# Reading the moving columns of three matrix products from the last to the first

## The chip, the cores and the metric

The kernel runs on one core of one Trainium2 chip. The metric is the device time of one execution in microseconds (us), as the median of several runs; lower is better. Besides these runs there is one execution taken by the hardware profiler, and all rows shown here come from that one.

## The reference

Windowed attention with a distance bias feeds a channel mix (a feed-forward block with token shift). Cut to what matters:

```python
B, H, S, D = 4, 8, 768, 64            # attention; x has 512 features
x = attention(q, k, v)                # -> (B, S, 512)
x_prev = shift x by one token
xk = mu_k * x + (1 - mu_k) * x_prev
xr = mu_r * x + (1 - mu_r) * x_prev
k = maximum(xk @ w_k, 0)              # w_k: 512 x 1024
v = (k * k) @ w_v                     # w_v: 1024 x 512
r = sigmoid(xr @ w_r)                 # w_r: 512 x 512
return r * v
```

The channel mix runs over 4 x 768 = 3072 tokens.

## The kernel before

The tokens are cut into 24 tiles of 128; two tiles form a chunk of 256, and the channel mix runs once for each of the 12 chunks. A main loop goes over the tiles: it loads q, k and v, forms scores (L421 to L425), takes the exponential (L431), transposes it (L461), multiplies it by v (L486), and a few steps later puts the chunk's channel mix in small pieces (a Python generator, `run_ffn`) between the pieces of the attention of later tiles. The final order of the instructions on each engine is set when the program is built, by a planner that lays the work out along a timeline of its own estimates.

All products of the channel mix are in split form: each operand is a high part and a low part in the 4-byte type fp32r, and `three` (L527 to L530) adds three matmuls into one sum in PSUM: high x high, high x low, low x high. So each line, L528, L529 and L530, holds a third of the matmuls. There are three products:

- **kp** (L546 to L554): weights of w_k are held in the array, the tokens of `xk` move past it, 256 columns each time. One PSUM tile takes two such sums (2 x 256). Four tiles for a chunk.
- **z** (L532 to L538): 128 tokens of `xr` are held, the 512 columns of w_r move. Two tiles for a chunk.
- **vps** (L573 to L579): 128 tokens of `kkh`/`kkl` (the square of the rectified kp, high and low) are held, the 512 columns of w_v move. Two tiles for a chunk; in the last chunk the second tile is done in two halves of 256 columns.

The sums of all three share the pool `ps_f`, three PSUM tiles that are handed out in turn. They are read by these four instructions: ScalarE takes the rectified kp (L555), VectorE multiplies it by kp (L556), ScalarE takes the sigmoid of z (L568), VectorE multiplies vps by it (L580). L557 and L558 then split the square into the high and low part that vps needs; these read SBUF only. The results go out by DMA (L581).

Two lines outside the channel mix serve as yardsticks later: L230, which in the first 35 us multiplies an identity by 512 columns of plain fp32, and L262/L264, which test the weights' raw 8-byte words late in the kernel and read every second 4-byte word.

Of the kernel before, what the change touches and what calls it, by code (L numbers as in the profile page):

```python
# [14 lines left out]
AF = mybir.ActivationFunctionType  # L15
# [47 lines left out]
def tile_biased_attention_channel_mix(ctx: ExitStack, tc: tile.TileContext, qT, kT, v, n_sizes, mu_kr, w_k, w_v, w_r, q_rows, k_rows, v_rows, slopes, out):  # L63
    nc = tc.nc
    vec, act, pool, pe = nc.vector, nc.scalar, nc.gpsimd, nc.tensor
# [27 lines left out]
    wts = {}  # L93
# [56 lines left out]
    for h in range(H):  # L150
        c = -8.0 * 2.0 ** -(h + 1)
# [15 lines left out]
    for h in range(H):  # L167
        c = -8.0 * 2.0 ** -(h + 1)
# [72 lines left out]
    def range_load():  # L241
        n = len(words_again)
        if n == 20:
            return
        name, src, j = w_steps[n // 2]
        if n % 2:
            raw = p4k.tile([128, 512, 2], I32, tag="t4k", name=f"again_{n}")
        else:
            raw = q_pool.tile([128, 512, 2], I32, tag=("qh", "ql")[n // 2 % 2], name=f"again_{n}")
        at, o = divmod((j * 2 + n % 2) * 512 // 512 * 1024 + n % 1 * 1024, 2048 if name == "k" else 1024)  # L250
        nc.sync.dma_start(raw.rearrange("p n w -> p (n w)"), src[at * 128 : (at + 1) * 128, o : o + 1024])
        words_again.append(raw)

    def range_test(behind_vec, behind_act):
        n = tested[0]
        if n == len(words_again):
            return
        tested[0] += 1
        raw = words_again[n]
        low, top = raw[:, :, 0], raw[:, :, 1]  # L260
        with tc.issue_after(behind_vec.ins):
            vec.tensor_scalar(low, top, 27, 15, op0=ALU.logical_shift_right, op1=ALU.bitwise_and)  # L262
        with tc.issue_after(behind_act.ins):
            act.activation(top.bitcast(F32), low, AF.Abs, bias=middle, accum_out=odd[:, n : n + 1])  # L264

    def range_worst():
        vec.reduce_max(worst[:, 0:1], odd, axis=AX.X)
        row = ps_f.tile([128, 512], F32, name="row", tag="f")
        pe.matmul(row[0:1, 0:128], worst[:, 0:1], ident, start=True, stop=True)
        vec.reduce_max(worst[0:1, 1:2], row[0:1, 0:128], axis=AX.X)  # L270
# [22 lines left out]
    def weights_need(n):  # L293
        weights_go(n, n)
# [211 lines left out]
    def part(pool, tag, n):  # L506
        t = pool.tile([128, n * 256 + GAP.get(tag, 0)], F32R, name=tag, tag=tag)
        return t[:, 0 : n * 256].rearrange("p (a q) -> p a q", a=n)
# [15 lines left out]
    def channel_mix(xk, xr, out_rows, f_pool, f2_pool, ps_f, more=False, final=False):  # L524
        kkh, kkl = (part(f_pool, f"kk_{p}", 8) for p in ("hi", "lo"))

        def three(o, sh, sl, mh, ml, first, last):  # L527
            pe.matmul(o, sh, mh, start=first, stop=False)  # L528
            pe.matmul(o, sh, ml, start=False, stop=False)  # L529
            pe.matmul(o, sl, mh, start=False, stop=last)  # L530

        def z_of(i):  # L532
            z = ps_f.tile([128, 512], F32, name="z", tag="f")
            c = slice(i * 128, (i + 1) * 128)
            for k in range(4):
                three(z, xr[0][:, k, c], xr[1][:, k, c], *wts["r", k], k == 0, k == 3)
                yield
            sig = f2_pool.tile([128, 512], F32, name="sig", tag="f2")  # L538
            sigs.append((z, sig))

        sigs = []
        for fp in range(4):
            weights_need(4)
            ps = ps_f.tile([128, 512], F32, name="kp", tag="f")
            for u in range(2):
                f = slice((2 * fp + u) * 128, (2 * fp + u + 1) * 128)  # L546
                o = ps[:, u * 256 : (u + 1) * 256]
                for k in range(4):
                    hi, lo = wts["k", k]
                    three(o, hi[:, f], lo[:, f], xk[0][:, k, :], xk[1][:, k, :], k == 0, k == 3)  # L550
                    if k % 2:
                        yield
            kk = f2_pool.tile([128, 2, 256], F32, name="kk", tag="f2")
            pv = ps.rearrange("p (a q) -> p a q", a=2)  # L554
            act.activation(kk, pv, AF.Relu)  # L555
            vec.tensor_mul(kk, pv, kk)  # L556
            high = act.copy(kkh[:, 2 * fp : 2 * fp + 2, :], kk)  # L557
            rest = vec.tensor_sub(kkl[:, 2 * fp : 2 * fp + 2, :], kk, kkh[:, 2 * fp : 2 * fp + 2, :])  # L558
            if more:
                for i in range(3):  # L560
                    range_load()
                for i in range(3):
                    range_test(rest, high)
        weights_need(6)
        for i in range(2):
            yield from z_of(i)
        for z, sig in sigs:
            act.activation(sig, z, AF.Sigmoid)  # L568
        for i in range(2):
            c = slice(i * 128, (i + 1) * 128)  # L570
            sig = sigs[i][1]
            ends = (0, 256, 512) if final and i else (0, 512)
            for a, b in zip(ends, ends[1:]):  # L573
                vp = ps_f.tile([128, 512], F32, name="vps", tag="f")
                for f in range(8):
                    weights_need(7 + f // 2)
                    hi, lo = wts["v", f]
                    three(vp[:, a:b], kkh[:, f, c], kkl[:, f, c], hi[:, a:b], lo[:, a:b], f == 0, f == 7)
                    yield  # L579
                vec.tensor_mul(sig[:, a:b], vp[:, a:b], sig[:, a:b])  # L580
                nc.sync.dma_start(out_rows(i)[:, a:b] if final and i else out_rows(i), sig[:, a:b])  # L581
            if more and i == 0 and tested[0] == 20:
                range_worst()

    def ffn(c):
        xt = state["x", c]
        xk = mix(xt[:, :, 1:257], xt[:, :, 0:256], "k", p4k, f_pool, c < PLAN.get("MA", 1))
        xr = mix(xt[:, :, 1:257], xt[:, :, 0:256], "r", p4k, f_pool, c < PLAN.get("MA", 1))
        return channel_mix(xk, xr, lambda i: out[(2 * c + i) * 128 : (2 * c + i + 1) * 128, :], f_pool, f2_pool, ps_f, c >= 10, c == NCHUNK - 1)
# [84 lines left out]
    def wide():  # L674
        weights_any()
        with ExitStack() as g:
# [85 lines left out]
            with tc.For_i(0, B, 1) as b:  # L762
                for c in range(3):
                    xt = work.tile([128, 4, 257], F32, name="g_x", tag="g_x")
                    src = rows[ds(b, 1)].rearrange("b p a s -> p (b a) s")
                    if c:
                        nc.sync.dma_start(xt, src[:, :, 256 * c - 1 : 256 * c + 256])
                    else:
                        pool.memset(xt[:, :, 0:1], 0.0)
                        nc.sync.dma_start(xt[:, :, 1:257], src[:, :, 0:256])  # L770
                    xk = mix(xt[:, :, 1:257], xt[:, :, 0:256], "k", work, work)
                    xr = mix(xt[:, :, 1:257], xt[:, :, 0:256], "r", work, work)

                    def out_rows(i):
                        return rows_out[ds(b, 1), (2 * c + i) * 128 : (2 * c + i + 1) * 128, :].rearrange("b s d -> (b s) d")

                    for _ in channel_mix(xk, xr, out_rows, work, work4, ps_f):
                        pass
# [63 lines left out]
```

## Time and profile before

| | us |
|---|---|
| median of 3 runs | 501.81 |
| the three runs | 504.63, 501.81, 500.86 |
| the profiled execution | 499.25 |
| its span, first to last instruction | 497.5 |
| TensorE busy (matmuls) in the span | 485.3 |
| VectorE busy | 350.4 |
| ScalarE busy | 329.2 |
| GpSimd busy | 205.9 |

The span is what the trace shows in rows; the profiled execution's own time is 1.75 us longer and lies 0.5% below the median of the runs. Engines work side by side, so the busy times don't add up to the span. A matmul's row lasts longer than the distance to the next matmul's start, since they are pipelined: what a matmul costs TensorE is the distance from one start to the next.

### The profile page before, as it was taken

How to read it: one execution, taken by the hardware profiler on the slowest of the kernel's cores; microseconds unless marked ns; L12 is line 12 of the kernel's file. 1: busy time of each engine (PE TensorE's matmuls, PEld its weight loads, DVE VectorE, ACT ScalarE, POOL GpSimd, SP SyncE). 2: the span in 40 equal slices, each digit the busy share in tenths (PEclk: the TensorE clock that was granted, in tenths of full speed). 3: DMA queues.
4: the chain of work that ended last, by engine and by line, in shares of the span. 5: the costliest groups of instructions: out<-in, count | busy, mean ns of one | idle time of the engine just before them, and what ended most of it. 6: DMA issues, size and time to landing. Idle time of an engine off the chain costs nothing.

```text
span 497.5 us, 10274 instructions
## 1 busy us (share of the span) xinstructions
PE 485.3 (98%) x3614; PEld 431.7 (87%) x3614; DVE 350.4 (70%) x839; ACT 329.2 (66%) x842; POOL 205.9 (41%) x339
## 2 busy tenths in 40 slices
PE   7999999899999999999999999999999999999995
PEld 5687997698988998998998998998998998988984
DVE  7999996677677677677687676677678665456431
ACT  8899866346287578567478477577587587595450
POOL 4211047337355544554655645644655634203000
PEclk9999999999999999999999999999999999999999
DMA  7997331650615306405405405405505125674301
GB/s 253 366 313 306 80 83 40 155 138 5 167 31 148 94 17 166 108 1 164 124 6 149 119 1 159 133 2 141 148 2 131 56 52 172 195 254 169 135 35 51
DMA packets 22587, 60.59 MB, mean 122 GB/s; under 512 B 3296, under 2 KB 4576, under 8 KB 22016
## 3 DMA queue, kind: packets, MB, share of 16 engines
q1 hardware_dynamic: 22384, 59.85, 40.2%
q8 instruction: 31, 0.51, 0.4%
q14 instruction: 28, 0.23, 0.2%
q10 hardware_dynamic: 144, 0.00, 0.0%
HBM read 53.55 MB, written 6.29 MB: 120 GB/s over the span
## 4 chain that ended last, share of the span: by engine, by line
PE 88%; DVE 6%; ACT 2%; DMA 1%; issue 1%; POOL 0%; SPq 0%; DVEq 0%; POOLq 0%; ACTq 0%
PE kp L528 9%; PE kp L529 9%; PE kp L530 9%; PE vps L528 8%; PE vps L530 8%; PE vps L529 8%; PE av L486 7%; PE t L461 7%; PE z L528 4%; PE z L529 4%; PE z L530 4%; PE s L425 3%; PE s L424 3%; PE s L422 2%; PE s L421 2%; PE rest L230 1%
## 5 line engine op out<-in xcount | busy, mean ns | idle before, releaser
L449 POOL TENSOR_SCALAR e<-e,r 128x232 f32<-128x232 f32 (+1 forms) x144 | 68.6, 495 | 129.3 <-DVE r L443 91.9
L431 ACT ACTIVATE e<-e,nmax 128x232 f32<-128x232 f32 (+1 forms) x192 | 89.6, 469 | 34.2 <-DVE nmax L430 33.6
L528 PE MATMUL kp<-xk_hi,wk 128*128 128x256 f32 x384 | 108.0, 282 | 1.8 <-DVE sig L580 1.8
L529 PE MATMUL kp<-xk_lo,wk 128*128 128x256 f32 x384 | 107.3, 280 | 0.1
L530 PE MATMUL kp<-xk_hi,wk 128*128 128x256 f32 x384 | 107.2, 279 | 0.0
L430 DVE CUSTOM_DVE_ANT_0 e<-s,pat 128x232 f32<-128x232 f32 (+1 forms) x192 | 64.2, 373 | 28.0 <-PE s L425 25.9
L528 PE MATMUL vps<-wv,kk_hi 128*128 128x512 f32 (+1 forms) x200 | 76.8, 385 | 0.2 <-ACT wv L216 0.2
L530 PE MATMUL vps<-wv,kk_lo 128*128 128x512 f32 (+1 forms) x200 | 76.6, 383 | 0.0
L529 PE MATMUL vps<-wv,kk_hi 128*128 128x512 f32 (+1 forms) x200 | 76.4, 382 | 0.0
L528 PEld LDWEIGHTS kp<-xk_hi,wk 128*128 128x128 f32 x384 | 72.0, 188 | 3.0 <-DVE sig L580 2.1
L529 PEld LDWEIGHTS kp<-xk_lo,wk 128*128 128x128 f32 x384 | 72.1, 188 | 1.2 <-DVE xk_lo L521 0.8
L530 PEld LDWEIGHTS kp<-xk_hi,wk 128*128 128x128 f32 x384 | 72.1, 188 | 0.0
L465 ACT COPY et<-t 128x256 f32<-128x256 f32 (+1 forms) x176 | 53.3, 355 | 25.1 <-PE t L461 24.9
L461 PE MATMUL t<-ident,e 128*128 128x128 f32 x352 | 54.4, 275 | 0.4 <-ACT et L465 0.3
L556 DVE TENSOR_TENSOR kk<-kp,kk 128x512 f32<-128x512 f32 x48 | 32.9, 688 | 30.8 <-ACT kk L555 30.4
L558 DVE TENSOR_TENSOR kk_lo<-kk,kk_hi 128x512 fp32r<-128x512 f32 x48 | 36.5, 764 | 22.8 <-ACT kk_hi L557 22.0
L461 PEld LDWEIGHTS t<-ident,e 128*128 128x128 f32 x352 | 40.3, 136 | 6.1 <-ACT et L465 0.6
L557 ACT CAST kk_hi<-kk 128x512 fp32r<-128x512 f32 x48 | 29.7, 622 | 22.4 <-DVE kk L556 22.4
L530 PEld LDWEIGHTS vps<-wv,kk_lo 128*128 128x128 f32 x200 | 37.6, 188 | 7.5
L528 PEld LDWEIGHTS vps<-wv,kk_hi 128*128 128x128 f32 x200 | 37.6, 189 | 7.0 <-ACT wv L216 0.4
L529 PEld LDWEIGHTS vps<-wv,kk_hi 128*128 128x128 f32 x200 | 37.7, 189 | 6.5
L400 DVE TENSOR_TENSOR ql<-qraw,qh 128x1024 fp32r<-128x1024 f32 x18 | 32.8, 1825 | 14.5 <-POOL qh L297 14.5
(119 smaller groups left out, 1075.1 us busy)
## 6 DMA issues: line engine op xcount, KB each, us to landing
qraw<-in_qT_dram SPq DMA_DIRECT2D x36, 256.0 KB
kraw<-in_kT_dram SPq DMA_DIRECT2D x36, 256.0 KB
out_dram<-sig SPq DMA_DIRECT2D x23, 256.0 KB
va<-in_v_dram SPq DMA_DIRECT2D x20, 240.0 KB
vb<-in_v_dram SPq DMA_DIRECT2D x20, 208.0 KB
w<-in_w_k_dram SPq DMA_DIRECT2D x4, 1024.0 KB
w<-in_w_v_dram SPq DMA_DIRECT2D x4, 1024.0 KB
again<-in_w_k_dram SPq DMA_DIRECT2D x8, 512.0 KB
```

The source lines that it names most:

```text
L400: vec.tensor_sub(ql, s["qr"], qh)
L430: biased[n, hp] = vec.tensor_tensor_reduce(out=e[:, :w], in0=o, in1=p[:, h, :], op0=ALU.add, op1=ALU.min, scale=-0.125, scalar=3.0e38, acc ...
L431: act.activation(e[:, :w], e[:, :w], AF.Exp, bias=s["nmax"][:, h : h + 1], scale=-1.0, accum_out=s["sum"][:, h : h + 1])
L449: pool.tensor_scalar(e[:, :w], e[:, :w], r[:, u : u + 1], 1.0, op0=ALU.mult, op1=ALU.mult)
L461: s["turned"] = pe.transpose(pt[0:p, c : c + 128], e[:, k * 128 : k * 128 + p], ident)
L465: act.copy(dst, pt[0:p, k * 256 : k * 256 + 256].rearrange("p (u q) -> p u q", u=2)[:, :, q:128])
L486: pe.matmul(o, vt[:, h * 64 : (h + 1) * 64], et[0:p, c : c + 128 - q], start=k == 0, stop=k == nb - 1)
L528: pe.matmul(o, sh, mh, start=first, stop=False)
L529: pe.matmul(o, sh, ml, start=False, stop=False)
L530: pe.matmul(o, sl, mh, start=False, stop=last)
L556: vec.tensor_mul(kk, pv, kk)
L558: rest = vec.tensor_sub(kkl[:, 2 * fp : 2 * fp + 2, :], kk, kkh[:, 2 * fp : 2 * fp + 2, :])
```

## The change

The moving operand of every matmul of the channel mix is read from its last column to its first (`[:, ::-1]`, a step of -1 element). The sums therefore stand in PSUM in reverse order of columns, and the four instructions that read these sums read them backwards too, so that everything that is written to SBUF has the order it had. Number and sizes of instructions, the operands held in the array, the buffers and the DMAs are as before.

```diff
@@ z_of
-                three(z, xr[0][:, k, c], xr[1][:, k, c], *wts["r", k], k == 0, k == 3)
+                three(z, xr[0][:, k, c], xr[1][:, k, c], wts["r", k][0][:, ::-1], wts["r", k][1][:, ::-1], k == 0, k == 3)
@@ kp
-                    three(o, hi[:, f], lo[:, f], xk[0][:, k, :], xk[1][:, k, :], k == 0, k == 3)
+                    three(o, hi[:, f], lo[:, f], xk[0][:, k, ::-1], xk[1][:, k, ::-1], k == 0, k == 3)
@@
-            pv = ps.rearrange("p (a q) -> p a q", a=2)
+            pv = ps.rearrange("p (a q) -> p a q", a=2)[:, :, ::-1]
             act.activation(kk, pv, AF.Relu)
             vec.tensor_mul(kk, pv, kk)
@@
-            act.activation(sig, z, AF.Sigmoid)
+            act.activation(sig, z[:, ::-1], AF.Sigmoid)
@@ vps
-                    three(vp[:, a:b], kkh[:, f, c], kkl[:, f, c], hi[:, a:b], lo[:, a:b], f == 0, f == 7)
+                    three(vp[:, a:b], kkh[:, f, c], kkl[:, f, c], hi[:, a:b][:, ::-1], lo[:, a:b][:, ::-1], f == 0, f == 7)
                     yield
-                vec.tensor_mul(sig[:, a:b], vp[:, a:b], sig[:, a:b])
+                vec.tensor_mul(sig[:, a:b], vp[:, a:b][:, ::-1], sig[:, a:b])
```

## Rows read from the trace of the kernel before

**Rows 1.** The profile's first part: busy time, share of the span, instructions.

```profile
PE 485.3 (98%) x3614; PEld 431.7 (87%) x3614; DVE 350.4 (70%) x839; ACT 329.2 (66%) x842; POOL 205.9 (41%) x339
```

**Rows 2.** Busy time of each engine by stretch (window, length, engines with instruction counts, clock).

```profile
core 0: us, PE busy (x) PEld busy (x) DVE busy (x) ACT busy (x) POOL busy (x), PEclk, DMA share, GB/s
0.00:100.00 100.00, 93.49 (x716) 77.50 (x717) 88.70 (x230) 75.45 (x219) 32.22 (x55) 1.00 0.63 200
100.00:475.00 375.00, 375.00 (x2805) 339.88 (x2804) 256.90 (x598) 248.66 (x612) 173.68 (x285) 1.00 0.37 107
475.00:497.50 22.50, 16.83 (x97) 14.31 (x95) 4.85 (x12) 5.07 (x13) 0.00 (x0) 0.95 0.08 28
```

**Rows 3.** The chain that ended last: shares of the span by engine.

```profile
PE 88%; DVE 6%; ACT 2%; DMA 1%; issue 1%; POOL 0%; SPq 0%; DVEq 0%; POOLq 0%; ACTq 0%
```

**Rows 4.** Groups by line and shape: the matmuls of L528 and counts of vps.

```profile
L528 PE MATMUL kp<-xk_hi,wk 128*128 128x256 f32 x384 | 108.0, 282 | 1.8 <-DVE sig L580 1.8
...
L528 PE MATMUL z<-wr,xr_hi 128*128 128x512 f32 x96 | 38.1, 397 | 0.0
...
L528 PE MATMUL vps<-wv,kk_hi 128*128 128x512 f32 x184 | 72.2, 393 | 0.2 <-ACT wv L216 0.2
...
L528 PE MATMUL vps<-wv,kk_hi x200: 277/389/497, 78.7 to 491.3; 128*128 128x512 f32 x92, 128*128 128x256 f32 x8
```

**Rows 5.** TensorE in order of time: start, duration (us); kp and z.

```profile
250.88 0.28 PE L528 MATMUL kp<-xk_hi,wk 128*128 128x256 f32 x1
...
253.00 0.28 PE L528 MATMUL kp<-xk_hi,wk 128*128 128x256 f32 x1
...
255.40 0.40 PE L530 MATMUL z<-wr,xr_lo 128*128 128x512 f32 x1
...
258.14 0.39 PE L530 MATMUL z<-wr,xr_lo 128*128 128x512 f32 x1
```

**Rows 6.** The yardstick L230: four in a row on TensorE, and its durations.

```profile
19.36 1.98 PE L230 MATMUL rest<-wa,ident 128*128 128x512 f32 x4
...
L230 PE MATMUL rest<-wa,ident x12: 592/592/697, 19.4 to 33.1; 128*128 128x512 f32 x12
```

**Rows 7.** The four readers of the sums: durations min/median/max in ns.

```profile
L555 ACT ACTIVATE kk<-kp x48: 574/588/618, 57.3 to 475.8; 128x512 f32<-128x512 f32 x48
L556 DVE TENSOR_TENSOR kk<-kp,kk x48: 674/692/693, 61.7 to 476.4; 128x512 f32<-128x512 f32 x48
L568 ACT ACTIVATE sig<-z x24: 582/598/602, 76.7 to 480.2; 128x512 f32<-128x512 f32 x24
L580 DVE TENSOR_TENSOR sig<-vps,sig x25: 425/682/693, 97.0 to 491.9; 128x512 f32<-128x512 f32 x23, 128x256 f32<-128x256 f32 x2
```

**Rows 8.** Instructions that read every second word: durations of L262 and L264.

```profile
L262 DVE TENSOR_SCALAR again<-again x20: 421/423/428, 435.5 to 477.9; 128x512 int32<-128x512 int32 x20
...
L264 ACT ACTIVATE again<-again,middle x20: 730/766/797, 436.6 to 479.3; 128x512 f32<-128x512 int32 x20
```

**Rows 9.** Life of a PSUM tile: its last kp matmul, its last reader, its next user.

```profile
253.24 0.28 PE L530 MATMUL kp<-xk_hi,wk 128*128 128x256 f32 x1
...
255.16 0.69 DVE L556 TENSOR_TENSOR kk<-kp,kk 128x512 f32<-128x512 f32 x1 [0.74 <-ACT kk L555]
...
263.46 0.39 PE L528 MATMUL vps<-wv,kk_hi 128*128 128x512 f32 x1
```

**Rows 10.** Whom TensorE waited for, longest first (total us, times, longest).

```profile
PE kp L528 <- DVE sig L580: 1.8, 1, 1.8
```

**Rows 11.** The end of the kernel: the last reader of a sum.

```profile
491.86 0.42 DVE L580 TENSOR_TENSOR sig<-vps,sig 128x256 f32<-128x256 f32 x1 [2.38 <-PE vps L530]
```

**Rows 12.** Instructions on kp (PE PEld DVE ACT), then on vps (PE PEld DVE), one stretch.

```profile
60.00:100.00 40.00, 9.50 (x72) 8.69 (x72) 2.64 (x4) 1.80 (x3) 1.00 0.44 101
...
60.00:100.00 40.00, 11.65 (x48) 8.79 (x48) 1.27 (x2) 1.00 0.44 101
```

## The prediction

> **What bounds the kernel now.** I read the busy times first, then the stretches, the chain that ended last, the groups of TensorE's lines, and last TensorE in order of time. TensorE is busy for 485.3 of 497.5 us, VectorE for 350.4 and ScalarE for 329.2 [rows 1]. The share alone would not say that TensorE is the bound, since the rows of pipelined matmuls overlap. The stretches do: from 100 to 475 us TensorE has no gap at all (375.00 of 375.00), at a granted clock of 1.00, which is the upper of its two levels, 2.4 GHz [rows 2]. The chain agrees with 88% on TensorE [rows 3]. In the first 100 us TensorE idles for 6.5 us, while VectorE is busy for 88.7 [rows 2]: only there do the other engines set the pace.
>
> So whatever changes the distance from one matmul to the next goes into the time in full. There is no cover. The distances: 18 kp matmuls (256 columns) go from 250.88 to 253.00, 118 ns each; 12 z matmuls (512 columns) from 255.40 to 258.14, 228 ns each [rows 5]. That is 0.45 ns for a column. Twice 118 less 228 leaves some 7 ns that don't grow with the columns.
>
> **How much is touched.** Each of L528 to L530 has 384 kp, 96 z and 200 vps matmuls, 184 of these with 512 columns and 16 with 256 [rows 4] (the fourth row keeps that proportion, 92 to 8). Three lines: 3 x (384 + 16) = 1200 matmuls of 256 columns and 3 x (96 + 184) = 840 of 512, 2040 in all. At 118 and 228 ns they take 141.6 + 191.5 = 333 us, two thirds of the span.
>
> **Edit 1, the moving operand backwards.** Nothing is added or taken away: same count, columns, operands held in the array. The only price is what a step of -1 does to the rate at which columns come out of SBUF. No row of before reads a moving operand with any step but +1, so I bound it from both sides.
> - Below: the part that could go is the 7 ns beside the columns. 2040 x 7 ns = 14 us. Nothing in the rows ties these 7 ns to the direction of reading, so I take no gain.
> - Above: the nearest row in which 512 columns of 4 bytes go by more slowly is L230, plain fp32. Four in a row take 1.98 us, the last of them 0.592, so (1.98 - 0.592) / 3 = 463 ns each [rows 6]: 235 ns over z's 228, half that for 256 columns. If a backward read cost as much: 840 x 0.235 + 1200 x 0.117 = 197 + 140 = 338 us.
>
> Between these ends I take zero. The one kind of row that shows reading with a step other than 1 stands with zero: L262 on VectorE reads and writes every second word, 512 of them in 423 ns, where L556 needs 692 ns for 512 words that lie side by side (an operation with two sources, from PSUM) [rows 7, 8]. A stream of 4-byte words is thus not slow merely for a step that isn't +1; and a backward step leaves the same words side by side, each read once. That is another engine's read, so the upper end stays as a rival.
>
> Two rules speak to this. The Trainium skill's page Advanced Engine Details and Errata, section SBUF Cachelines, says that SBUF has lines of 16 bytes, and that accesses run at full speed while at least two fall on the same line: columns of 4 bytes meet a line four times in either direction, so by it the sum stays at zero. The Trainium skill's page Vector Engine (DVE) Microarchitecture Reference, section 5.2 Measured stream behaviour on trn2, says that VectorE's ports keep full rate only in runs of two or more adjacent words that start on an 8-byte boundary, with 1.73 against 1.054 ns for a column where one source hops at every element; its section 5.1 lists a negative step as not measured. Read strictly, and carried over to TensorE, a backward stream has no such run; an estimate from the page's ratio would add 0.64 x 333 = 213 us. No row here shows which of the two holds for a step of -1.
>
> **Edit 2, the readers of PSUM backwards.** 48 L555 (588 ns), 48 L556 (692), 24 L568 (598) and 25 L580 (682) [rows 7]. Below: no gain, their columns stay 512. Above, ScalarE: L264 reads and writes every second word and takes 766 ns for 512, 178 more than L555, though part of that is its other operands [rows 7, 8]. Above, VectorE: no row has a PSUM read out of order; I let the instruction double, +0.69 us, as L230 does. I take zero for both, with L262 as the reason again.
>
> What hides it if it isn't zero: a PSUM tile comes back to TensorE after two other tiles. Take the kp tile whose last matmul starts at 253.24 and ends at 253.52; its last reader ends at 255.16 + 0.69 = 255.85; the vps that takes its place starts at 263.46 [rows 9]: 7.6 us to spare. Where two kp tiles follow instead, they alone take 48 x 118 ns = 5.7 us, and the readers were done 2.3 us after the sum: 3.3 us to spare against at most 0.18 + 0.69 = 0.87. From 100 to 475 us VectorE has 118 us idle and ScalarE 126 [rows 2], and the bounds ask for 73 x 0.69 = 50 and 72 x 0.18 = 13 in the whole kernel. Without cover are the first 100 us: TensorE's only wait of over 1.5 us for a reader is 1.8 us of a kp matmul for L580 [rows 10]; VectorE has there 4 reads of kp and 2 of vps, ScalarE 3 of kp [rows 12]. All of them end-on: 6 x 0.69 + 3 x 0.18 = 4.7 us. The last L580, half a tile in 0.42 us, stands bare before the last DMA [rows 11]: 0.4 more. So edit 2 costs between 0 and 5 us.
>
> **Sum.** 499.25 us of the profiled execution + 0 + 0 = 499.25. That execution is 2.6 us (0.5%) below the median of the runs, so the forecast in the median's terms is 501.8, put down as 502.
>
> **Rivals.**
> - *B, the backward read halves TensorE's rate.* For it: TensorE takes a 4-byte column in each 0.45 ns, the fastest stream in the kernel, and L230 shows that 512 columns can take twice as long. Against: L262. Price 338 us: 499 + 338 = 837, about 840 in the median's terms. It decides early: 5 us, the 1% from which a measurement of this kernel can be told from no change, is 5 / 2040 = 2.5 ns for a matmul, and any smaller penalty lands between 507 and 840. That is the other side. The strict reading of the Trainium skill's section 5.2 (Vector Engine (DVE) Microarchitecture Reference) is this rival's rule.
> - *C, the readers slow down, the columns don't.* 0 to 5 us by the sum above, in the first 100 us; with its upper bound 504 to 505, in the median's terms 507. It needs nearly the whole bound to leave the 1%. A longer wait like that of [rows 10] may repeat itself once or twice, so up to 511.
> - *D, the order moves.* The planner orders instructions by its own estimates. If it prices a backward read differently, pieces of the attention move against the channel mix. In the 375 us without a gap that is worth nothing; before 100 us it can give back at most the 6.5 us of idle time [rows 2]: 499.25 - 6.5 = 493, or 495 in the median's terms. It can as well lose a few, which I count with C. Against a gain: all 6.5 would have to go, and part of it comes before the first data.
> - *The change doesn't do what it says*: steps that are folded away when the program is built would give 502 too, and can't be told from the forecast by time.
>
> **How the numbers follow.** Forecast within 1%: 0.75. B: 0.16, since only an engine with a different read speaks against it. C with the loss part of D: 0.05. D as a gain: 0.04. The range reaches from 495 (D's bound) to 512 (C's); it leaves out B, 0.16, and little else. Faster by over 1%: 0.04; within 1%: 0.75; slower: 0.16 + 0.05 = 0.21.
>
> **What would show it.** Forecast right: kp starts 118 ns apart and z 228, TensorE without a gap from 100 to 475 us, L555, L556, L568 and L580 within some 20 ns of [rows 7], counts of [rows 4] unchanged. B: distances of z above 230 ns and of kp above 120, with every other engine's share fallen. C: the readers' rows longer, and TensorE's waits for L580 or L556 grown in the first 100 us. D: other starts of the first kp and z, and another idle time before 100 us. The forecast is wrong if the distances move by more than 2.5 ns; its weakest step is that a VectorE row stands for how TensorE reads.

## The result, and the profile after

| | before | after |
|---|---|---|
| median of the runs (us) | 501.61 | 508.56 |
| lowest and highest | 500.86, 504.63 | 506.65, 508.62 |
| profiled execution, its span | 499.25, 497.5 | 506.65, 504.8 |

The ratio of the runs is 1.0116, 95% interval 1.0076 to 1.0155. By it the change makes the kernel 1.2% slower, 5.8 us; the two medians lie 7.0 us apart. The time lies inside the predicted range, but past the 1% that was forecast.

The profile after, in the order in which that of before was read. The busy part, the stretches and the chain, which answer to [rows 1 to 3]:

```profile
PE 493.9 (98%) x3614; PEld 436.7 (87%) x3614; DVE 352.4 (70%) x839; ACT 331.0 (66%) x842; POOL 205.0 (41%) x339
```
```profile
0.00:100.00 100.00, 94.57 (x700) 78.05 (x701) 87.27 (x228) 75.95 (x219) 30.52 (x53) 1.00 0.61 195
100.00:475.00 375.00, 375.00 (x2762) 337.16 (x2762) 255.66 (x589) 244.19 (x599) 174.43 (x287) 1.00 0.38 106
475.00:504.80 29.80, 24.34 (x156) 21.47 (x155) 9.45 (x22) 10.88 (x25) 0.00 (x0) 0.95 0.12 39
```
```profile
PE 92%; DVE 4%; ACT 1%; DMA 1%; issue 0%; POOL 0%; SPq 0%; POOLq 0%; ACTq 0%
```

Same counts, the first 100 us hardly changed (5.4 us idle where it was 6.5), still no gap from 100 to 475 us at a granted clock of 1.00, but 2762 matmuls in those 375 us where there were 2805: each takes longer. TensorE in order of time, to set beside [rows 5]; the first two rows are 26 kp distances apart, the last two 12 z distances:

```profile
250.22 0.28 PE L528 MATMUL kp<-xk_hi,wk 128*128 128x256 f32 x1
...
253.34 0.28 PE L530 MATMUL kp<-xk_hi,wk 128*128 128x256 f32 x1
...
259.17 0.40 PE L528 MATMUL z<-wr,xr_hi 128*128 128x512 f32 x1
...
261.97 0.40 PE L528 MATMUL z<-wr,xr_hi 128*128 128x512 f32 x1
```

kp: 3.12 / 26 = 120.0 ns (118 before). z: 2.80 / 12 = 233.3 ns (228 before). The readers and the one long wait, which answer to [rows 7] and [rows 10]:

```profile
L555 ACT ACTIVATE kk<-kp x48: 569/590/610, 58.5 to 483.1; 128x512 f32<-128x512 f32 x48
L556 DVE TENSOR_TENSOR kk<-kp,kk x48: 676/692/694, 62.9 to 483.7; 128x512 f32<-128x512 f32 x48
...
L568 ACT ACTIVATE sig<-z x24: 580/597/600, 78.4 to 487.7; 128x512 f32<-128x512 f32 x24
...
L580 DVE TENSOR_TENSOR sig<-vps,sig x25: 425/683/694, 99.0 to 499.4; 128x512 f32<-128x512 f32 x23, 128x256 f32<-128x256 f32 x2
```
```profile
PE kp L528 <- DVE sig L580: 2.1, 1, 2.1
```

The medians are 590, 692, 597 and 683 ns where they were 588, 692, 598 and 682, and the wait is 2.1 us where it was 1.8.

**Where the time went.** The order of the instructions is the same on every engine, so the k-th matmul of one trace can be set beside the k-th of the other. The last one starts 7.5 us later. By the product whose matmul begins a distance, the distances of kp grow by 2.6 us in all, those of vps by 2.4, those of z by 1.2: 6.3 us, spread evenly. Another 1.2 us is there by the 50th matmul, before the channel mix begins, at the start of this one execution (its scatter is shown at the end). For a single matmul, the mean of the distances between neighbours of the same product (the longest twentieth, around breaks, left out) says: kp 117.3 to 119.8 ns, z 229.0 to 233.4, vps 228.6 to 233.3. The 48 vps matmuls of 256 columns went the other way, 119.8 to 118.2.

### The profile page after: what moved, and what is told of

Same layout as the page of the kernel before. It is cut to its first block, busy times and chain, and to the rows that moved or that the text cites. A ratio compares the mean times of both kernels' runs of the same rounds, so it can differ in the third digit from the quotient of the medians.

```text
span 504.8 us, 10276 instructions
## 1 busy us (share of the span) xinstructions
PE 493.9 (98%) x3614; PEld 436.7 (87%) x3614; DVE 352.4 (70%) x839; ACT 331.0 (66%) x842; POOL 205.0 (41%) x339
## 4 chain that ended last, share of the span: by engine, by line
PE 92%; DVE 4%; ACT 1%; DMA 1%; issue 0%; POOL 0%; SPq 0%; POOLq 0%; ACTq 0%
PE kp L528 9%; PE kp L529 9%; PE kp L530 9%; PE vps L528 8%; PE vps L529 8%; PE vps L530 8%; PE av L486 8%; PE t L461 7%; PE z L528 5%; PE z L529 4%; PE z L530 4%; PE s L425 3%; PE s L424 3%; PE s L422 2%; PE s L421 2%; PE rest L230 1%
## 5 line engine op out<-in xcount | busy, mean ns | idle before, releaser
L528 PE MATMUL kp<-xk_hi,wk 128*128 128x256 f32 x384 | 109.1, 285 | 2.1 <-DVE sig L580 2.1
L529 PE MATMUL kp<-xk_lo,wk 128*128 128x256 f32 x384 | 108.5, 283 | 0.2 <-DVE xk_lo L521 0.2
L530 PE MATMUL kp<-xk_hi,wk 128*128 128x256 f32 x384 | 108.3, 282 | 0.0
L528 PE MATMUL vps<-wv,kk_hi 128*128 128x512 f32 (+1 forms) x200 | 78.0, 391 | 0.0
L529 PE MATMUL vps<-wv,kk_hi 128*128 128x512 f32 (+1 forms) x200 | 77.7, 388 | 0.0
L530 PE MATMUL vps<-wv,kk_lo 128*128 128x512 f32 (+1 forms) x200 | 77.7, 388 | 0.0
L528 PEld LDWEIGHTS kp<-xk_hi,wk 128*128 128x128 f32 x384 | 72.1, 188 | 3.3 <-DVE sig L580 2.4
L528 PEld LDWEIGHTS vps<-wv,kk_hi 128*128 128x128 f32 x200 | 37.7, 189 | 7.3 <-issue 0.2
L400 DVE TENSOR_TENSOR ql<-qraw,qh 128x1024 fp32r<-128x1024 f32 x18 | 34.2, 1899 | 12.4 <-POOL qh L297 12.4
```

Of the source, the lines that this page charges most:

```text
L400: vec.tensor_sub(ql, s["qr"], qh)
```

## The experiments

**One part alone, and the readers alone.**

The first run takes kp alone, with its readers:

```diff
-  three(o, hi[:, f], lo[:, f], xk[0][:, k, :], xk[1][:, k, :], k == 0, k == 3)
+  three(o, hi[:, f], lo[:, f], xk[0][:, k, ::-1], xk[1][:, k, ::-1], k == 0, k == 3)
   ...
-  pv = ps.rearrange("p (a q) -> p a q", a=2)
+  pv = ps.rearrange("p (a q) -> p a q", a=2)[:, :, ::-1]
```

The second takes the lines of z and vps with their two readers, as the change has them, and leaves kp. The third has the four readers backward and all matmuls forward, so its results stand in reverse order within their blocks of columns.

> Only kp's moving operand (1152 matmuls of 256 columns) and its two readers go backwards. Theory S (each backward matmul costs TensorE a little more, in step with its columns): the distance between kp matmuls is 120.0 ns as in the changed kernel, against 117.7 before, z and vps stay at 228 to 229; 1152 x 2.3 ns = +2.7 us, about 504 us. Rival R (the readers of PSUM cost it): kp's distance stays 117.7 and the waits on L555 and L556 grow. Rival K (the clock's start alone): 501 to 502 with all distances as before.

> Only z's and vps's moving operands (840 matmuls of 512 columns, 48 of 256) and their readers go backwards. Theory S: z and vps at 233 ns against 228.5 before, kp at 117.7; 840 x 4.8 ns = +4.0 us, about 506 us; with e1 the two add up to the whole change's 7 us. Rival R: the distances stay at 228.5. Rival K: 501 to 502.

> The moving operands go forward as before, only the four readers of PSUM go backwards; the results are therefore written in reverse order within each block, which leaves the amount of work the same. Theory S: all distances as before, time as before (501 to 502.5). Rival R: the whole of the change's 7 us, 508 us.

Measured: kp alone 1.0036 (1.0004 to 1.0067), z and vps alone 1.0054 (1.0023 to 1.0084), the readers alone 0.9995 (0.9965 to 1.0025). The groups of L528 in the three traces (a matmul's mean duration moves with its distance: 282 ns for kp, 397 for z and 393 for vps before [rows 4]); first kp alone, then z and vps alone, then the readers alone:

```profile
L528 PE MATMUL kp<-xk_hi,wk 128*128 128x256 f32 x384 | 109.5, 286 | 1.9 <-DVE sig L580 1.9
...
L528 PE MATMUL vps<-wv,kk_hi 128*128 128x512 f32 x184 | 72.2, 393 | 0.0
...
L528 PE MATMUL z<-wr,xr_hi 128*128 128x512 f32 x96 | 38.0, 396 | 0.0
```
```profile
L528 PE MATMUL kp<-xk_hi,wk 128*128 128x256 f32 x384 | 108.7, 284 | 2.2 <-DVE sig L580 2.2
...
L528 PE MATMUL vps<-wv,kk_hi 128*128 128x512 f32 x184 | 73.3, 400 | 0.0
...
L528 PE MATMUL z<-wr,xr_hi 128*128 128x512 f32 x96 | 38.6, 402 | 0.0
```
```profile
L528 PE MATMUL kp<-xk_hi,wk 128*128 128x256 f32 x384 | 108.0, 282 | 2.2 <-DVE sig L580 2.2
...
L528 PE MATMUL vps<-wv,kk_hi 128*128 128x512 f32 x184 | 72.2, 393 | 0.2 <-ACT wv L216 0.2
...
L528 PE MATMUL z<-wr,xr_hi 128*128 128x512 f32 x96 | 38.1, 397 | 0.0
```

The longer distances go with the product that is read backwards, and only with it: kp 119.9 ns in the first run, z 233.4 and vps 233.3 in the second; all as before in the third. In the second run kp, unedited, became a little faster: 12 of its 41 longer runs without a break hold 113.3 ns, where 3 of 42 did before, and its mean falls to 116.8; what can pick such a distance is taken up below. Edit 2 costs nothing that these runs can tell, edit 1 carries the whole cost, and the parts add up: 0.36% + 0.54% = 0.9%, within the interval of the whole.

**TensorE alone.** Is it the direction, or something in the kernel beside it? A kernel with series of 36 matmuls of the same kind and no other work on TensorE (attention and channel mix are left out); the granted clock is 1.00 from 24 to 184 us. The moving operand is 512 or 256 columns forward or backward, or blocks of 2, 4 or 16 columns in reverse order and forward inside a block, or every second column forward or backward.

```diff
+ for i in range(36):
+     pe.matmul(t, wt[:, (i % 16) * 128 : (i % 16) * 128 + 128], moving, start=i == 0, stop=i == 35)
```

> None of the reference's computation: TensorE alone runs series of 36 matmuls in fp32r, each series with one way of reading the moving operand, while all other engines are idle. Series f512 and b512 read the same 512 columns forward and backward, f256 and b256 the same 256; blkb, blkd and blkp read blocks of 2, 4 and 16 columns from the last block to the first, forward inside a block; foff and boff begin 1, 4 or 16 columns later; stepb and stepc read every second column forward and backward; the series ending in same hold one and the same weights. Theory S1 (the direction itself costs, whatever else goes on): b512 is some 5 ns and b256 some 2.3 ns slower than f512 and f256 in every pair. Rival S2 (the direction matters only against the address at which the weights or other traffic are read): f512 and b512 differ by under 1 ns here or change order with the offset. For the line-based rule: blkd and blkp lie with f512 if the order inside a line matters, with b512 if the order of the lines does. Step 2: no more than f512 if columns are simply fetched one by one, near double if two neighbours are fetched together.

One row for each series; the distance is the next series' start less its own, by 36. L55 and L58 are 256 columns forward and backward, L61 and L64 512 columns with the same weights each time, L85 and L91 reversed blocks of 2 and 16, L94 and L97 every second column, L100 and L103 again 512 columns forward and backward:

```profile
33.30 4.49 PE L55 MATMUL f<-mv,wt 128*128 128x256 f32 x36
37.62 4.43 PE L58 MATMUL b<-mv,wt 128*128 128x256 f32 x36
41.88 8.35 PE L61 MATMUL f512same<-mv,wt 128*128 128x512 f32 x36
50.07 8.57 PE L64 MATMUL b512same<-mv,wt 128*128 128x512 f32 x36
58.48 8.69 PE L67 MATMUL foff<-mv,wt 128*128 128x512 f32 x36
...
108.89 8.57 PE L85 MATMUL blkb<-mv,wt 128*128 128x512 f32 x36
...
125.69 8.57 PE L91 MATMUL blkp<-mv,wt 128*128 128x512 f32 x36
134.10 16.41 PE L94 MATMUL stepb<-mv,wt 128*128 128x512 f32 x36
150.32 16.98 PE L97 MATMUL stepc<-mv,wt 128*128 128x512 f32 x36
167.12 8.37 PE L100 MATMUL fend<-mv,wt 128*128 128x512 f32 x36
175.32 8.57 PE L103 MATMUL bend<-mv,wt 128*128 128x512 f32 x36
```

512 columns: forward 8.19 / 36 = 227.5 ns, backward 8.41 / 36 = 233.6 (226.7 to 227.4 and 233.3 inside a series). Blocks in reverse order cost as much as single columns: 8.41 / 36 for blocks of 16. Every second column takes 16.22 / 36 = 451 ns, twice the time. But 256 columns are faster backward here, 118.3 against 120.0 ns, the opposite of kp in the kernel. So the direction alone isn't the price. The series in which the moving columns begin 1, 4 or 16 columns further (L67 is the first) gave a second hint: forward 236.7, 231.7 and 228.9 ns, backward 235.6, 233.3 and 233.3.

**The place.** Three theories: D, each direction has its price; M, the place where the moving operand begins in its row of 64 columns (256 bytes) sets it; W, the place of the moving operand against that of the weights does (both come out of SBUF at the same time: from 100 to 475 us loads of weights run for 339.88 of the 375 us in which matmuls have no gap [rows 2]). Series of 24 on TensorE alone, with the weights, the moving operand or both moved, and with fewer weight columns held, each forward and backward.

```diff
- pe.matmul(t[:, 0:n], wt[:, k : k + 128], mv[:, 0:n], ...)
+ pe.matmul(t[0:m, 0:n], wt[:, k + wo : k + wo + m], mv[:, mo : mo + n], ...)
```

> None of the reference's computation: series of 24 matmuls in fp32r with all other engines idle. Three kinds of series, each forward and backward. First, 512 columns past 128, 64 or 32 held columns. Second, the weights begin 2, 4, 8, 16, 32 or 64 columns later, with 512 (long) and 256 (short) moving columns. Third, the moving operand begins 2 to 128 columns later. In e4 the same 512 columns took 226.7 ns forward and 233.3 backward, 256 took 120.1 forward and 118.3 backward. Theory W (the two reads that TensorE makes, of the weights and of the moving operand, get in each other's way, and the direction only changes where they meet): with 32 held columns both directions come near 216 ns, the bf16 distance in e4; and the distances of both directions change with the weights' offset, so that forward and backward change places at some offsets. Rival M (the moving read alone sets it): halving or quartering the held columns changes nothing, and the weights' offset neither; only the moving offset does. Rival D (a fixed price of the direction): backward is slower than forward by the same amount in every pair of 512.

Rows with the weights 4 and 64 columns further, and with both 4 and both 16 further (512 columns, forward):

```profile
66.98 5.77 PE L49 MATMUL wofour_long_fwd<-mv,wt 128*128 128x512 f32 x24
...
134.65 5.63 PE L49 MATMUL wosixtyfour_long_fwd<-mv,wt 128*128 128x512 f32 x24
```
```profile
235.86 5.68 PE L49 MATMUL bothfour_long_fwd<-mv,wt 128*128 128x512 f32 x24
...
244.18 5.66 PE L49 MATMUL bothsixteen_long_fwd<-mv,wt 128*128 128x512 f32 x24
```

Forward, the advantage is gone when the weights alone are moved by 4 columns (inside the series 233.4 ns), and back when they are moved by 64 (227.2) or when both are moved by 16 (228.3). So M falls, since the weights' place counts; D falls, since forward takes anything from 226.7 to 233.4. Backward stays at 233.3 nearly throughout (235.6 with the moving operand 2 further, 236.7 where either is moved by 32). W holds in this part, but not in its strict form: with both moved by 4 columns, so that one stands against the other as at first, forward takes 230.0, so each place counts also by itself. And what W said of fewer held columns didn't come: with 128, 64 and 32 of them forward takes 227.7, 229.7 and 231.6, backward always 233.3.

**The place in the kernel.** By the addresses of the built program, which no row shows, the weights of all three products begin at column 16 of such a row in the kernel before; the moving columns of z and vps too, those of kp at column 32. Moving the tiles of xk by 48 columns gives kp the place of z and vps. The order and number of instructions stay.

```diff
- GAP = {"kk_hi": 16, "xk_lo": 112}
+ GAP = {"kk_hi": 16, "xk_hi": 48, "xk_lo": 64}
+ SKIP = {"xk_hi": 48}
```

(`part` starts the tile at that column.) In the first run all is forward, in the second kp alone is backward.

> Everything forward as before, but xk's two tiles lie 48 columns (192 bytes) further on, so that kp's moving columns begin in the same place of a 256-byte row as its weights; before they began 16 columns after them, as worked out from the addresses of the built program. Theory W (the two reads of TensorE meet, and address as well as direction shifts where): kp forward goes from 117.7 to 120.0 ns, as f256 did in e4, z and vps stay; 1152 x 2.3 ns = +2.7 us. Rival D (the direction has a price of its own, addresses don't matter in the kernel): 117.7 ns and no change.

> As e1 (only kp and its readers backward), with xk moved by the same 48 columns as in e6. Theory W: kp backward takes 118.3 ns as b256 did in e4, below the 120.0 of e1 and below the 120.0 expected of e6, so that at this address the backward read is the faster one; against before 1152 x 0.6 ns = +0.7 us, some 2 us under e1. Rival D: 120.0 ns as in e1, +2.7 us.

One run of kp matmuls from each trace, 21 distances forward and 29 backward:

```profile
254.42 0.29 PE L530 MATMUL kp<-xk_hi,wk 128*128 128x256 f32 x1
...
256.93 0.28 PE L530 MATMUL kp<-xk_hi,wk 128*128 128x256 f32 x1
```
```profile
252.55 0.28 PE L530 MATMUL kp<-xk_hi,wk 128*128 128x256 f32 x1
...
255.99 0.28 PE L532 MATMUL kp<-xk_hi,wk 128*128 128x256 f32 x1
```

They take 2.51 / 21 = 119.5 and 3.44 / 29 = 118.6 ns. Over the whole trace kp goes forward from 117.3 to 119.6 ns, ratio 1.0041 (1.0013 to 1.007); backward at the same place it takes 118.2, ratio 1.0027 (1.0001 to 1.0054). A move in SBUF that leaves the program as it was costs as much as reading kp backwards did (1.0036), and by the distances backward is the faster direction there, as it was with TensorE alone; the times of the two moved kernels can't be told apart. The 48 short vps matmuls, which begin at that same relative place, had shown it in the first comparison.

**All places.** TensorE alone again: 256 columns at each even place against the weights, 512 at every eighth (letters a to z, then A to F, stand for 0, 2, ... 62 columns past the weights' place).

```diff
+ for o in range(32):
+     series(f"short_fwd_{code[o]}", 128, 0, 2 * o, 256, False)
+     series(f"short_bwd_{code[o]}", 128, 0, 2 * o, 256, True)
  ... (the same with 512 columns, o in steps of 4)
```

> None of the reference's computation: series of 24 fp32r matmuls as in e5, all other engines idle, weights begin at the same place of a 256-byte row as in the kernel. The moving operand of 256 columns begins 0, 2, 4 ... 62 columns further on (letters a to z, then A to F), forward and backward in turn; then 512 columns in steps of 8. Theory W: both directions vary by several ns with the place, neither is always the faster one at 256 columns; at letter i (16 columns on, the kernel's place) forward is near 117.7 and backward near 120.0, at a near 120 and 118.3. Rival D: backward is slower at each place by the same 2.3 ns.

kp's place (i, 16 columns past the weights) and one of the places with the shortest time (y, 48 past; c and s, 4 and 36 past, hold the same 113.3 ns):

```profile
62.85 3.00 PE L51 MATMUL short_fwd_i<-mv,wt 128*128 128x256 f32 x24
65.68 3.04 PE L51 MATMUL short_bwd_i<-mv,wt 128*128 128x256 f32 x24
...
154.38 2.90 PE L51 MATMUL short_fwd_y<-mv,wt 128*128 128x256 f32 x24
157.12 2.99 PE L51 MATMUL short_bwd_y<-mv,wt 128*128 128x256 f32 x24
```

Inside the series, i takes 117.8 forward and 119.9 backward, as in the kernel; y takes 113.35 and 117.9. Forward ranges from 113.35 to 121, backward from 117.65 to 120. Of 512 columns only forward at the weights' own place and 16 past it is below 232 (227.7 and 228.9); backward is 233.3 at all eight, also 32 past the weights, where it took 236.7 in the series before, in which both tiles began 48 columns earlier.

**The best place in the kernel.** By that, a kp at y's place should gain. Three runs: all products forward at this place, the whole change at this place, and the changed kernel itself once more.

```diff
- GAP = {"kk_hi": 16, "xk_lo": 112}
+ GAP = {"kk_hi": 16, "xk_hi": 32, "xk_lo": 80}
+ SKIP = {"xk_hi": 32}
```

> Everything runs forward, as before the change; only the tiles of xk lie 32 four-byte columns further in SBUF, so that the first moving column of a kp matmul stands 48 columns past the place of the weights in its row of 64 columns (32 less 16 before the change, so 16). Everything is computed. Theory W (what a forward matmul takes is set by where its moving columns begin against its weights, within 256 bytes): kp starts 113.4 ns apart, as the series with that place did when TensorE ran alone, where it was 117.3 in the kernel before; 1152 matmuls by 4 ns are 4.6 us, so about 497 us and a ratio of 0.990 to the kernel before. Theory D (forward and backward have each a price of their own and the place has none): kp stays at 117.3 and the ratio is 1.000. z and vps stay at 228 to 229 by both.

> The whole change (all three products and their readers backward) with the tiles of xk 32 four-byte columns further, as in the run beside it. Everything is computed. Theory W: backward kp at this place starts 117.9 ns apart, where the changed kernel had 119.8; 1152 by 2 ns are 2.3 us, so a ratio to the kernel before of 1.005 to 1.009, and against the forward kernel at the same place the change of direction would cost 4.5 ns on kp and 4.5 ns on z and vps, some 9 us. Theory D: kp stays at 119.8, z and vps at 233.3, the ratio stays that of the changed kernel, about 1.012.

> The changed kernel itself, beside the two others, for a closer ratio to the kernel before. Everything is computed. By the distances of its trace (kp 2.5 ns and z and vps 4.5 ns longer, 1152 and 840 matmuls) it is 6.6 us longer, a ratio of 1.011 to 1.013; if part of the first difference was the start of the single profiled run, it is nearer to 1.009.

Ratios to the kernel before: 0.9962 (0.9932 to 0.9991), 1.008 (1.005 to 1.011) and, for the changed kernel, 1.0124 (1.0084 to 1.0163). The last confirms the result; its distances sum to 6.3 us more than those of before, as in the first trace. In the second, backward kp starts 118.1 ns apart, where 117.9 was expected. Forward at y's place is faster than the kernel before, but by 2 us and not by the 5 expected: kp's mean is 115.5, not 113.4. The trace says why. Two runs of kp matmuls of e9_forward_48, one behind the other: 24 distances between the first pair of rows, 20 between the second.

```profile
251.19 0.28 PE L530 MATMUL kp<-xk_hi,wk 128*128 128x256 f32 x1
...
254.02 0.28 PE L530 MATMUL kp<-xk_hi,wk 128*128 128x256 f32 x1
...
255.60 0.28 PE L530 MATMUL kp<-xk_hi,wk 128*128 128x256 f32 x1
...
257.87 0.28 PE L532 MATMUL kp<-xk_hi,wk 128*128 128x256 f32 x1
```

2.83 / 24 = 117.9 ns, then 2.27 / 20 = 113.5, with the same operands at the same places. Of the 42 longer runs of kp matmuls in this trace 20 hold 113 to 114 ns and 22 hold 118: a run settles at one of two distances and keeps it until pieces of the attention break it.

**The moment of the start.** Five kinds of series, each behind three matmuls of another width, from 128 to 248 columns (p, letters a to p in steps of 8).

```diff
+ for j in range(3):
+     pe.matmul(u[:, 0:p], wt[:, 0:128], mv[:, 0:p], start=True, stop=True)
  for i in range(24): ...
```

> TensorE alone; nothing of the attention or the channel mix is computed. Series of 24 fp32r matmuls like those before, each behind three matmuls of another width (128 to 248 columns in steps of 8, letters a to p), which shift the moment at which the series begins. Places as in the kernel: short series of 256 columns 48 columns past the weights forward and backward, kp's old place (16 past) forward, long ones of 512 at the weights' own place forward and backward. Theory S (the place only allows a distance, and the moment at which a run begins against what runs ahead of it picks one of a few that then hold): short forward holds about 113.4 ns behind some widths and about 118 behind others, as in the kernel with this place, where runs of both kinds stand side by side; long forward starts with distances of 231 to 238 and settles at 226.7 after some 5 to 10, and long backward is at 233.3 from the first. Theory P (the place alone decides): short forward 113.4 behind every width, and the runs of 118 in the kernel came from what the other engines do.

256 columns at y's place behind widths a and f; then the 512 columns behind width a, forward (the 2nd to the 11th matmul, then the 11th to the 24th) and backward (the 2nd to the 10th, then the 10th to the 24th):

```profile
17.02 2.87 PE L53 MATMUL short_fwd_a<-mv,wt 128*128 128x256 f32 x23
```
```profile
123.12 2.54 PE L53 MATMUL short_fwd_f<-mv,wt 128*128 128x256 f32 x21
```
```profile
26.63 2.47 PE L53 MATMUL long_fwd_a<-mv,wt 128*128 128x512 f32 x10
```
```profile
28.71 3.33 PE L53 MATMUL long_fwd_a<-mv,wt 128*128 128x512 f32 x14
```
```profile
32.45 2.27 PE L53 MATMUL long_bwd_a<-mv,wt 128*128 128x512 f32 x9
```
```profile
34.32 3.66 PE L53 MATMUL long_bwd_a<-mv,wt 128*128 128x512 f32 x15
```

With the last row's own 0.28 or 0.39 us taken off: (2.87 - 0.28) / 22 = 117.7 ns behind a, (2.54 - 0.28) / 20 = 113 behind f. At y's place 4 of 16 widths give 113.3 to 113.8 and 12 give 117.8; at kp's old place 6 of 16 give 113.3 and the others 117.6 to 118. Backward at y's place is at 117.8 behind 15 widths and at 120 behind one. So both places allow 113.3, and what runs ahead picks; the widths change the moment of the start and nothing within the series, but that it is the moment as such isn't shown. Forward 512 first takes (2.47 - 0.39) / 9 = 231 ns and then (3.33 - 0.39) / 13 = 226: it settles after up to a dozen matmuls, behind each of the 16 widths. Backward 512 takes (2.27 - 0.40) / 8 = 234 and (3.66 - 0.40) / 14 = 233 from the start, behind each width. Theory P (the place alone decides) falls, and with it the reading of a single series of 256 columns in the sweep as a property of its place. What stands without it are the kernels, over 1152 matmuls each: kp forward takes 119.6 at the weights' own place, and kp backward 119.8, 118.2 and 118.1 at 16, 0 and 48 past the weights, where the sweep's series settle at 120.0, 118.3 and 117.8.

## Why the prediction was right in its range and wrong in its sum

**The bound was read rightly.** TensorE has no cover: 6.3 us more of distances came out as 5.8 us more of time by the ratio (3.8 to 7.8 by its interval).

**That the time fell inside the range was luck.** The upper end, 512, is rival C's, slower readers, and they didn't slow down. What came is a small form of rival B, which the range left out by name; B's band begins at 507, below C's end, so the two overlap.

**Edit 1 is the step that failed: the term was taken as zero, and it is 6.3 us** (2040 matmuls by 3.1 ns, above the 2.5 ns that the prediction named as its point of decision). Both ends, -14 and +338 us, hold it; what failed is the choice between them. It rested on L262, a VectorE row, for how TensorE reads, which the prediction called its weakest step. With TensorE alone, every second column doubles the time (451 ns against 227), where L262 showed no such thing, so that row bore no witness. A row of TensorE's own for another step didn't exist in the trace before; so nothing on record tied the term to zero rather than to a small price, and 2.5 ns for a matmul were enough to leave the forecast.

**Rival B came, in its small form.** The kernel is slower through TensorE's distances and lands at the bottom of B's band (507 to 840): 2% on the 512 columns and on kp instead of 100%. Of B's signs one came, z above 230 (233.4); kp stayed just below 120 (119.8), and the other engines' shares didn't fall (70, 66 and 41% as before). B's cause, a halved rate, didn't come, and the price isn't one of the direction alone: kp's hangs on where its tile lies. The Trainium skill's page Vector Engine (DVE) Microarchitecture Reference, section 5.2 Measured stream behaviour on trn2, which stood behind it, speaks of VectorE; carried over to TensorE it fits the step of 2 in kind (a factor of 2 here, 1.64 there) and not the step of -1. The Trainium skill's page Advanced Engine Details and Errata, section SBUF Cachelines, asks for two hits on a line of 16 bytes: that holds roughly for the step of -1 and for reversed blocks (within 3%), but a step of 2 meets each line twice and still takes 451 ns. So neither, carried over to TensorE's moving operand, gives all that was measured.

**Also missed:** that the 7 ns aren't a part beside the columns. Where both settle forward, 256 columns take 113.3 and 512 take 226.7, exactly twice; the 7 ns came from a kp run that held 118. And the row [rows 5] of z, 228 ns, was a mean of distances that are 228 to 236 after a break and end at 226.7. Two more readings were loose without bearing on the outcome: the four matmuls of [rows 6] start 533, 429 and 430 ns apart, and with 430 the upper end would be 291 us, not 338; and [rows 12] begin at 60 us, so that the first 100 us hold 5 reads of kp by ScalarE and 2 of z, not 3 of kp, and the bound of 4.7 us would be 5.4.

**Edit 2 at zero was right,** by e3_readers_only (0.9995, 0.9965 to 1.0025) and by the readers' medians. **Rival C** didn't come: the one wait grew by 0.3 us. **Rival D** didn't: the order is the same on every engine. **The change does what it says:** the distances moved for the products that were edited and for no other.

**What stays open.** Why a backward stream of 512 columns doesn't reach the settled distance of a forward one at any place tried, and why kp's backward stream takes 120 at its place in the kernel and 118 at the two others. That it depends on the places of the moving operand and the weights in 256 bytes, and on the moment of the start, points to the two reads of SBUF meeting; no run shows the meeting itself. The 1.2 us at the start isn't explained by the change.

## What to carry to other kernels

Where TensorE has no gap, a price of 1% of a matmul is a price in full, so a change to its operands' pattern can't be put at zero on another engine's row; measure it with TensorE alone, where a series of 36 takes 8 us, and with the operands at the kernel's own places: at another place the same 256 columns were faster backward (118.3 against 120.0). Compare then the distances by product in the whole trace, not the times: they showed 2 ns of 118 plainly where a dozen runs of kp alone just cleared no change (1.0004 to 1.0067). And try moves of an operand: 32 columns of free SBUF ahead of xk gained 0.4%, and 48 columns cost 0.4%, with no other change to the kernel.

## What the runs showed of the hardware that was not expected

- An fp32r matmul's distance depends on where its moving columns and its weights begin within 256 bytes, and on what runs ahead of the run: 113.3 to 121 ns for 256 columns, 226.7 to 236.7 for 512, with the same instructions and sizes.
- Every second column of 4 bytes halves TensorE's rate (451 ns for 512), backward a little more (467).
- The start of an execution scatters by almost as much as the change costs. The first profile of the changed kernel lost 1.2 us there, the second 6.1 us by the 100th matmul. The stretches of that second profile, and after them the same ones of the kernel before:

```profile
10.00:20.00 10.00, 5.59 (x45) 5.08 (x44) 6.87 (x28) 7.00 (x30) 1.79 (x2) 0.86 1.00 319
20.00:25.00 5.00, 5.00 (x34) 4.81 (x34) 3.14 (x13) 2.04 (x6) 0.00 (x0) 0.59 1.01 384
```
```profile
10.00:20.00 10.00, 9.52 (x83) 8.25 (x83) 9.24 (x39) 9.88 (x39) 1.79 (x2) 1.00 1.03 363
20.00:25.00 5.00, 5.00 (x34) 2.86 (x33) 4.80 (x8) 3.66 (x11) 1.14 (x1) 1.00 1.00 401
```

TensorE's granted clock was 0.86 and 0.59, part of the time at its lower level of 1.2 GHz, where it was 1.00 before; it had been busy for 5.6 of the 10 us ahead, where it was 9.5. e9_forward_48 shows the same (0.86 and 0.60 in these stretches). So a single span says little of a change of 1%; ratios of many runs and distances in the settled part do.
